# A GEGLU feed-forward kernel: x transposed by the loading transfers instead of by TensorE and VectorE

## The chip, the core and the metric

The kernel runs on one core of one Trainium2 chip. The metric is the device time of one execution in microseconds (us). Before the change the median of 3 runs is 299.68 us (299.42 to 299.73).

The core's parts have these names in the profile: PE is TensorE's matmul (PEld its weight load), DVE is VectorE, ACT is ScalarE, POOL is GpSimd, SP is SyncE, which only issues transfers here. A "q" behind a name (SPq) is that engine's instruction queue where it issues transfers. The transfers of all queues run on the same 16 DMA engines.

## The reference

```python
B, S, D, F = 32, 32, 1024, 3584      # 1024 tokens, all tensors bf16
def reference(x, w_gate, w_up, w_down):
    return (gelu(x @ w_gate) * (x @ w_up)) @ w_down
```

Two products contract over D = 1024, the third over F = 3584.

## The kernel before

It is a hand-ordered program: every engine has its own list of instructions, and semaphores (the `_Clock` objects) tie the lists together. Nothing is scheduled by a tool.

**First stage.** For each chunk m of 128 columns of F (28 chunks) and each group of tokens, TensorE forms gate and up, transposed (F on the partitions, tokens along the rows), in PSUM: 8 steps over the contraction (`dk`), each a matmul of a 128x128 weight block with `xT[:, dk, tokens]` (line 381). ScalarE applies gelu to the gate (line 439), VectorE multiplies with up into `hT` (line 479). The first 8 chunks ("big" weights) are done first for tokens 0 to 255 (parts 0 to 7), then for 256 to 511 (parts 8 to 15), with 256-column matmuls; then their tokens 512 to 1023 and all other chunks with 512-column matmuls. In parts 0 to 7 the loop over `dk` is outside (`together`): all eight chunks take step `dk` for gate and up, so that one weight piece feeds 8 matmuls. Steps 6 and 7 are done in two halves, and step 7 part by part (`one_by_one`). Each accumulates in its own half bank of PSUM.

**Second stage.** The product with `w_down` (line 418), 16 blocks of 128 tokens by 512 columns (the last one in two), each 28 steps; ScalarE and VectorE copy them out in turn, SyncE stores them.

**Where x comes from.** The matmuls need x with the contraction on the partitions. Before the change the contraction index is laid out as `(p k)`: partition p holds rows 8p to 8p+7 of the weights, step `dk` takes one of each eight. x is loaded in its own layout into space in `hT` that is not used yet, and turned in the core:
- tokens 0 to 255 (`xa`, two transfers of 256 KB, one on SyncE's and one on ScalarE's queue, line 292): steps 0 to 4 by ten TensorE matmuls with an identity (line 350), copied from PSUM to `xT` by three ScalarE instructions (line 432); steps 5 to 7 by sixteen VectorE transposes of 32x32 blocks (line 455). The identity is made by POOL (lines 313, 315).
- tokens 256 to 1023 (twelve transfers, half of them on each of two queues, line 283, issued once weight piece `wu` 5 has landed): twenty VectorE transposes (line 470), placed by hand between the VectorE multiplications (`mix`, line 187). Parts 8 to 11 are therefore done in 128-token halves for steps 0 to 3.

**The leading weights.** SyncE issues, one after the other, 16 pieces of 256 KB (line 288): `wg` 0, `wu` 0, `wg` 1, ... `wu` 7; piece k holds step k of the first 8 chunks. Later weights come in groups of four chunks, 1 MB a transfer, gate on SyncE's queue and up on POOL's (line 277); group 0 waits until the last x piece has landed (`gate_w`, line 303), the others until TensorE is done with the buffer. `w_down` is loaded in between (line 271).

**Warming.** Ten matmuls of ones (six of 512 columns, four of 128; line 390) come first on TensorE.

Of the kernel before, what the change touches and what calls it, by code (L numbers as in the profile page):

```python
# [5 lines left out]
P = 128  # L6
BF16 = mybir.dt.bfloat16
FP32 = mybir.dt.float32
ACTF = mybir.ActivationFunctionType
# [75 lines left out]
def bass_standalone__geglu_ffn__sampling_kernel(  # L85
# [13 lines left out]
    DK = D // P  # L99
# [26 lines left out]
    XC = N // 32  # L126
    XE = D // 4
    XA, XB, XC2 = (0, 256), (256, 512), (512, 1024)
    XB1, XB2 = (256, 384), (384, 512)
    XPIECES = [XB1, XB2, XC2]  # L130
    XA_PS = [(3, 0, 1), (4, 1, 3), (5, 3, 5)]
    XA_DVE = (5, 8)
# [25 lines left out]
    def together(ps_, k0, k1, tok=None):  # L158
        for dk in range(k0, k1):
            for key in ("G", "U"):  # L160
                for p in ps_:
                    steps.append((p, key, dk, tok))

    def one_by_one(ps_, k0):
        for p in ps_:
            for key in ("G", "U"):
                for dk in range(k0, DK):
                    steps.append((p, key, dk, None))

    for k0, k1 in ((0, 3), (3, XA_DVE[0])):  # L170
        for b in range(2):
            steps += [("X", b, dk) for dk in range(k0, k1)]
    for key, ps_ in (("G", (0, 1, 2, 3, 7, 6, 4)), ("U", (0, 1, 2, 3)), ("G", (5,)), ("U", (7, 6, 4, 5))):
        steps += [(p, key, 0, None) for p in ps_]
    together(range(0, 8), 1, 6)
    for half in (range(0, 4), range(4, 8)):
        together(half, 6, 7)
        one_by_one(half, 7)
    together(range(8, 12), 0, 4, XB1)
    together(range(8, 12), 0, 4, XB2)  # L180
    together(range(8, 12), 4, 6)
# [3 lines left out]

    dve_order = []
    mix = ("E0 E1 E2 A0 E3 A1 A2 A3 B0 B1 B2 B3 E4 D4 D5 E5 D6 D7 E6 E7 "
           "C0 E8 C1 E9 C2 E10 E11 C3 C4 E12 C5 E13 C6 C7 E14 E15")
    for w in mix.split():
        if w[0] == "E":  # L190
            dve_order.append(("E", int(w[1:])))
        else:
            dve_order.append(("T", int(w[1:])) + {"A": XB1, "B": XB2, "C": XC2, "D": XB}[w[0]])
    dve_order += [("E", p) for p in range(NSHORT, NPART)]
# [14 lines left out]
    xa_r = xf.rearrange("(b p) d -> p b d", p=P)  # L209
    x_r = xf.rearrange("(c i) (a e) -> a i c e", i=32, a=4)  # L210
    wg_r = w_gate.rearrange("(p k) f -> p k f", k=DK)
    wu_r = w_up.rearrange("(p k) f -> p k f", k=DK)
# [5 lines left out]
    C_POOL = _Clock("pool")  # L218
    Q_XA = [_Clock(f"xa{b}", 16) for b in range(2)]
    Q_X = {(q, s): _Clock(f"x{i}{s}", 16) for i, q in enumerate(XPIECES) for s in range(2)}  # L220
    Q_W0 = {(w, k): _Clock(f"{w}0k{k}", 16) for k in range(DK) for w in ("wg", "wu")}
# [5 lines left out]
    all_clocks = [C_PE, C_ACT, C_DVE, C_POOL, *Q_XA, *Q_X.values(), *Q_W0.values(), *Q_WG, *Q_WU,  # L227
# [4 lines left out]
    with ExitStack() as es:  # L232
# [6 lines left out]
        assert 8 * N == XC * XE  # L239
        xs = hT[:, FM - 8:FM, :].rearrange("p a (b e) -> p (a b) e", e=XE)  # L240
        xa = hT[:, FM - 10:FM - 8, :]
        ident = sb("ident", [P, P], BF16)
        diff = sb("diff", [P, P], mybir.dt.int32)
# [36 lines left out]
        def load_x(ew, eng, q, side):  # L280
            c0, c1 = q[0] // 32, q[1] // 32
            for a in (2 * side, 2 * side + 1):
                v = ew.do(lambda: eng.dma_start(
                    xs[32 * a:32 * (a + 1), c0:c1, :], x_r[a, :, c0:c1, :]), clock=Q_X[(q, side)])
            ctx.set(("x", q, side), v)

        def load_w0(ew, eng, w, k):
            ctx.set((w + "0", k), ew.do(lambda: eng.dma_start(  # L288
                big[w][:, k, :], w_r[w][:, k, 0:NBIG * P]), clock=Q_W0[(w, k)]))

        def early_loads(ew, eng, side):
            ctx.set(("xa", side), ew.do(lambda: eng.dma_start(  # L292
                xa[:, side, :], xa_r[:, side, :]), clock=Q_XA[side]))
            yield
            if side == 0:
                for k in range(DK):
                    for w in ("wg", "wu"):
                        load_w0(ew, eng, w, k)
            ew.wait(Q_W0[("wu", 5)], ctx.get(("wu0", 5)))
            for q in XPIECES:  # L300
                load_x(ew, eng, q, side)

        def gate_w(ew, j):
            if war[j] is None:
                for s in range(2):
                    ew.wait(Q_X[(XC2, s)], ctx.get(("x", XC2, s)))
                return -1
            ew.wait(C_PE, ctx.get(("U", last_part[war[j]])))
            return war[j]

        def prog_pool(eng):
            pool = _Eng(ctx, eng, C_POOL)
            v = pool.do(lambda: eng.iota(diff[:, :], pattern=[[1, P]], base=0, channel_multiplier=-1))
            pool.wait(C_POOL, v)
            ctx.set("ident", pool.do(lambda: eng.tensor_scalar(
                ident[:, :], diff[:, :], 0.0, None, ALU.is_equal)))
# [8 lines left out]
        def prog_sp(eng):  # L325
            sp = _Eng(ctx, eng, None)
            for _ in early_loads(sp, eng, 0):
                pass
# [15 lines left out]
        def turn_xa(pe, eng, b, dk):  # L344
            pe.wait(Q_XA[b], ctx.get(("xa", b)))
            j = next(j for j, (_, k0, k1) in enumerate(XA_PS) if k0 <= dk < k1)
            bank, k0, k1 = XA_PS[j]
            o = 256 * (dk - k0) + P * b
            last = dk == k1 - 1 and b == 1
            v = pe.do(lambda: eng.matmul(  # L350
                ps[:, bank, o:o + P],
                xa[:, b, :].rearrange("p (j k) -> p j k", k=DK)[:, :, dk],
                ident[:, :], start=(dk == k0 and b == 0), stop=last), mark=last)
            if last:
                ctx.set(("XP", j), v)

        def part_step(pe, eng, opened, i, key, dk, tok):
            m, t0, t1, gs, us = parts[i]
            w, (bank, f0, f1) = ("wg", gs) if key == "G" else ("wu", us)
            if tok is not None:  # L360
                f0, f1 = f0 + tok[0] - t0, f0 + tok[1] - t0
                t0, t1 = tok
            buf, slot, j = slot_of[m]
            if j is None:
                pe.wait(Q_W0[(w, dk)], ctx.get((w + "0", dk)))
            else:
                pe.wait((Q_WG if w == "wg" else Q_WU)[j], ctx.get((w, j)))
            if bank in bank_before[i]:
                pe.wait(C_DVE, ctx.get(("D", bank_before[i][bank])))
            for jx, (xbank, k0, k1) in enumerate(XA_PS):  # L370
                if t0 == XA[0] and (xbank == bank or k0 <= dk < k1):
                    pe.wait(C_ACT, ctx.get(("XA", jx)))
            if t0 == XA[0] and dk >= XA_DVE[0]:
                pe.wait(C_DVE, ctx.get("XD"))
            for q in XPIECES:
                if q[0] < t1 and t0 < q[1]:
                    pe.wait(C_DVE, ctx.get(("T", dk, q)))
# [12 lines left out]
        WARM = [512] * 6 + [128] * 4  # L390

        def prog_pe(eng):
# [4 lines left out]
            pe.wait(C_POOL, ctx.get("ident"))  # L397
            opened = set()
            for step in steps:
                if step[0] == "X":  # L400
                    turn_xa(pe, eng, *step[1:])
                else:
                    part_step(pe, eng, opened, *step)
# [22 lines left out]
        def prog_act(eng):  # L426
            act = _Eng(ctx, eng, C_ACT)
            act.do(lambda: eng.activation(warm[:, 0:1], const0, ACTF.Gelu_apprx_tanh))
            for _ in early_loads(act, eng, 1):
                for j, (bank, k0, k1) in enumerate(XA_PS):  # L430
                    act.wait(C_PE, ctx.get(("XP", j)))
                    ctx.set(("XA", j), act.do(lambda: eng.activation(  # L432
                        xT[:, k0:k1, XA[0]:XA[1]],
                        ps[:, bank, 0:256 * (k1 - k0)].rearrange("p (k t) -> p k t", t=256), ACTF.Copy)))
# [13 lines left out]
        def prog_dve(eng):  # L448
            dve = _Eng(ctx, eng, C_DVE)

            for b in range(2):
                dve.wait(Q_XA[b], ctx.get(("xa", b)))
            for q in range(4):
                for a in range(4):
                    v = dve.do(lambda: eng.transpose(  # L455
                        xT[32 * a:32 * (a + 1), XA_DVE[0]:XA_DVE[1], XA[0]:XA[1]].rearrange(
                            "p k (b t) -> p k b t", t=P)[:, :, :, 32 * q:32 * (q + 1)],
                        xa[32 * q:32 * (q + 1), :, :].rearrange(
                            "p b (j k) -> p k b j", k=DK)[:, XA_DVE[0]:XA_DVE[1], :, 32 * a:32 * (a + 1)]))
            ctx.set("XD", v)  # L460
            for what in dve_order:
                if what[0] == "T":
                    dk, q = what[1], what[2:]
                    landed = [r for r in XPIECES if q[0] <= r[0] < q[1]]
                    for r in landed:
                        for s in range(2):
                            dve.wait(Q_X[(r, s)], ctx.get(("x", r, s)))
                    src = xs[:, q[0] // 32:q[1] // 32, :].rearrange(
# [3 lines left out]
                    for r in landed:  # L472
                        ctx.set(("T", dk, r), v)
# [63 lines left out]
```

## Time and profile before

| what | from | number |
|---|---|---|
| median of 3 runs | times | 299.68 us |
| span of the profiled execution, first to last instruction | page | 298.2 us |
| median less span | worked out | 1.48 us |
| TensorE busy | page, part 1 | 294.9 us |
| VectorE / ScalarE busy | page, part 1 | 64.3 / 42.2 us |
| first-stage matmuls on the chain from 16.91 us | chain in order of time | 182.50 us |
| second-stage matmuls on the chain | chain in order of time | 96.78 us |
| granted TensorE clock | stretches | 1.00 throughout |
| SyncE's issue of a leading weight piece | line 288 | 0.42 to 0.61 us |
| issue of a piece of x behind the weights | line 283 | 0.33 to 1.33 us |

The time of the profiled execution as a whole is not given beside its span; the span is compared with the median.

The leading weight pieces of the same execution, us from the span's start. Issue is from the timeline, landing is issue plus the time to landing that line 288 shows in a window around the issue:

| piece | issue | landing | piece | issue | landing |
|---|---|---|---|---|---|
| wg 0 | 1.17 | 4.8 | wg 4 | 5.05 | 10.7 |
| wu 0 | 1.64 | 5.7 | wu 4 | 5.70 | 11.4 |
| wg 1 | 2.11 | 6.5 | wg 5 | 6.18 | 12.1 |
| wu 1 | 2.58 | 7.2 | wu 5 | 6.65 | 12.75 |
| wg 2 | 3.06 | 7.95 | wg 6 | 7.13 | 13.4 |
| wu 2 | 3.56 | 8.8 | wu 6 | 7.68 | 14.1 |
| wg 3 | 4.03 | 9.3 | wg 7 | 8.17 | 14.8 |
| wu 3 | 4.51 | 10.0 | wu 7 | 8.66 | 16.86 |

How to read it: a share of busy time is an average over the whole span. What a change is worth is read from the stage that it touches, and there from the wait that ends last. In a row of the timeline the first two numbers are start and duration in us; "x8" is the number of instructions merged into it, and what stands in brackets is how long the engine was idle before and what ended it. A row of the stretches gives start:end, length, the busy time of five engines, the granted clock, the DMA engines' busy share (which can exceed 1 where packets overlap) and GB/s.

### The profile page before, as it was taken

Reading aid. Unit: us, or ns where it says so; the run is one execution under the profiler, and the core shown is the slowest. Engines: PE = TensorE matmul, PEld = TensorE weight load, DVE = VectorE, ACT = ScalarE, POOL = GpSimd, SP = SyncE. Lnnn points to the kernel's source line nnn. Section 1 sums busy time; section 2 is a strip of 40 time slices with the busy share of each in tenths; the row PEclk is TensorE's granted clock in tenths of the full one; section 3 lists DMA queues with packets and bytes.
Section 4 is the critical chain, followed back from the end, with each engine's and each line's share of the span. In section 5 each row is a group of like instructions: output and inputs, shape, how many; then the busy total and the mean of one; then the engine's idle time right before and its main releaser. Section 6 shows DMA issues by size and latency. Waiting matters only on the chain.

```text
span 298.2 us, 3515 instructions
## 1 busy us (share of the span) xinstructions
PE 294.9 (99%) x1552; PEld 149.1 (50%) x1552; DVE 64.3 (22%) x108; ACT 42.2 (14%) x78; POOL 7.9 (3%) x14
## 2 busy tenths in 40 slices
PE   8999999999999999999999999999999999999997
PEld 5889644444444444444444444444444444444446
DVE  4669721111122111122111122110000000000000
ACT  3032211121111121111112111110000000000000
POOL 1001001020000002001000000000000000000000
DMA  7988004856009301943103000000000100010001
GB/s 258 391 197 263 22 2 133 289 186 240 0 0 294 131 0 31 372 162 92 51 0 141 0 2 0 0 0 20 18 18 20 35 18 18 20 35 18 18 20 35
DMA packets 17807, 26.43 MB, mean 89 GB/s; under 512 B 1025, under 2 KB 11393, under 8 KB 17793
## 3 DMA queue, kind: packets, MB, share of 16 engines
q1 hardware_dynamic: 13840, 16.78, 17.2%
q0 software_dynamic: 2176, 8.39, 7.9%
q10 hardware_dynamic: 1776, 1.05, 1.3%
q8 instruction: 12, 0.20, 0.3%
q14 instruction: 3, 0.02, 0.0%
HBM read 24.12 MB, written 2.10 MB: 88 GB/s over the span
## 4 chain that ended last, share of the span: by engine, by line
PE 94%; DMA 3%; SPq 2%; issue 0%; ACT 0%
PE ps L381 61%; PE ps L418 32%; DMA wubig<-in_w_up_dram 3%; SPq L288 2%; SPq L292 0%; ACT xT L445 0%
## 5 line engine op out<-in xcount | busy, mean ns | idle before, releaser
L418 PE MATMUL ps<-wd,hT 128*128 128x512 bf16 (+1 forms) x476 | 96.9, 366 | 0.0
L381 PE MATMUL ps<-xT,wubig 128*128 128x512 bf16 (+2 forms) x400 | 79.8, 336 | 0.3 <-DMA wubig<-in_w_up_dram 0.3
L381 PE MATMUL ps<-xT,wgbig 128*128 128x512 bf16 (+2 forms) x400 | 79.8, 336 | 0.2 <-ACT xT L432 0.2
L418 PEld LDWEIGHTS ps<-wd,hT 128*128 128x128 bf16 x476 | 46.6, 98 | 50.4
L479 DVE TENSOR_TENSOR hT<-tb,ps 128x512 bf16<-128x512 f32 (+1 forms) x64 | 39.0, 616 | 136.6 <-PE ps L381 136.6
L439 ACT ACTIVATE tb<-ps 128x512 f32<-128x512 f32 (+1 forms) x64 | 34.2, 544 | 158.4 <-PE ps L381 156.9
L381 PEld LDWEIGHTS ps<-xT,wubig 128*128 128x128 bf16 x400 | 38.1, 98 | 32.1 <-DMA wubig<-in_w_up_dram 0.7
L381 PEld LDWEIGHTS ps<-xT,wgbig 128*128 128x128 bf16 x400 | 38.0, 98 | 31.6 <-DMA wgbig<-in_w_gate_dram 0.3
L381 PE MATMUL ps<-xT,wgsmall 128*128 128x512 bf16 x128 | 30.2, 379 | 0.0
L381 PE MATMUL ps<-xT,wusmall 128*128 128x512 bf16 x128 | 30.2, 379 | 0.0
L485 DVE CAST xT<-ps 128x512 bf16<-128x512 f32 (+1 forms) x8 | 5.3, 658 | 88.1 <-PE ps L418 88.1
L381 PEld LDWEIGHTS ps<-xT,wusmall 128*128 128x128 bf16 x128 | 12.5, 98 | 15.1
L381 PEld LDWEIGHTS ps<-xT,wgsmall 128*128 128x128 bf16 x128 | 12.5, 98 | 15.1
L445 ACT ACTIVATE xT<-ps 128x512 bf16<-128x512 f32 (+1 forms) x9 | 5.2, 573 | 93.1 <-PE ps L418 93.1
L470 DVE STREAM_TRANSPOSE xT<-hT 128x128 bf16<-128x128 bf16 (+2 forms) x20 | 13.4, 714 | 0.0
L455 DVE STREAM_TRANSPOSE xT<-hT 32x192 bf16<-32x192 bf16 x16 | 8.3, 516 | 4.6 <-DMA hT<-in_x_dram 4.1
L277 POOL DMA_DIRECT2D wubig<-in_w_up_dram x3 | 2.7, 886 | 63.3 <-PE ps L381 63.3
L395 PE MATMUL ps<-const-bfloat16-1.0 128*128 128x512 bf16 (+1 forms) x10 | 3.1, 498 | 0.8 <-PEq L522 0.8
L277 POOL DMA_DIRECT2D wusmall<-in_w_up_dram x2 | 2.0, 992 | 47.3 <-PE ps L381 26.0
L271 POOL DMA_DIRECT2D wd<-in_w_down_dram x3 | 2.3, 764 | 19.1 <-PE ps L381 19.1
L395 PEld LDWEIGHTS ps<-const-bfloat16-1.0 128*128 128x128 bf16 x10 | 1.2, 139 | 2.4 <-issue 2.4
L432 ACT ACTIVATE xT<-ps 128x512 bf16<-128x512 f32 (+1 forms) x3 | 1.4, 526 | 2.2 <-PE ps L350 2.2
(10 smaller groups left out, 4.5 us busy)
## 6 DMA issues: line engine op xcount, KB each, us to landing
wd<-in_w_down_dram SPq DMA_DIRECT2D x4, 1024.0 KB, 11.5
wgbig<-in_w_gate_dram SPq DMA_DIRECT2D x3, 1024.0 KB, 5.6
wubig<-in_w_up_dram POOLq DMA_DIRECT2D x3, 1024.0 KB, 9.7
wd<-in_w_down_dram POOLq DMA_DIRECT2D x3, 1024.0 KB, 11.4
wgbig<-in_w_gate_dram SPq DMA_DIRECT2D x8, 256.0 KB, 5.5
wubig<-in_w_up_dram SPq DMA_DIRECT2D x8, 256.0 KB, 5.6
wgsmall<-in_w_gate_dram SPq DMA_DIRECT2D x2, 1024.0 KB, 5.8
wusmall<-in_w_up_dram POOLq DMA_DIRECT2D x2, 1024.0 KB, 9.7
```

Source lines behind the costliest of these rows:

```text
L271: ew.do(lambda: eng.dma_start(wd[:, a:b, :], wd_r[:, a:b, :]), clock=clock)
L277: ctx.set((w, j), ew.do(lambda: eng.dma_start(wbuf(w, buf)[:, :, 0:gsz * P], w_r[w][:, :, c0 * P:(c0 + gsz) * P]), clock=q))
L288: ctx.set((w + "0", k), ew.do(lambda: eng.dma_start(big[w][:, k, :], w_r[w][:, k, 0:NBIG * P]), clock=Q_W0[(w, k)]))
L381: v = pe.do(lambda: eng.matmul(ps[:, bank, f0:f1], wbuf(w, buf)[:, dk, slot * P:(slot + 1) * P], xT[:, dk, t0:t1], start=first, stop=last ...
L395: pe.do(lambda: eng.matmul(ps[:, 0, 0:n], ones_w, ones_x[:, 0:n], start=True, stop=True), mark=False)
L418: v = pe.do(lambda: eng.matmul(ps[:, b, 0:ncols], hT[:, m, tc * P:(tc + 1) * P], wd[:, m, col0:col0 + ncols], start=(m == 0), stop=(m == F ...
L439: ctx.set(("A", i), act.do(lambda: eng.activation(t_bufs[i % NTB][:, 0:t1 - t0], ps[:, gb, g0:g1], ACTF.Gelu_apprx_tanh)))
L445: ctx.set(("E", ji), act.do(lambda: eng.activation(osb[:, tc, col0:col0 + ncols], ps[:, b, 0:ncols], ACTF.Copy)))
L455: v = dve.do(lambda: eng.transpose(xT[32 * a:32 * (a + 1), XA_DVE[0]:XA_DVE[1], XA[0]:XA[1]].rearrange("p k (b t) -> p k b t", t=P)[:, :, ...
L470: v = dve.do(lambda: eng.transpose(xT[:, dk, q[0]:q[1]].rearrange("p (c i) -> p c i", i=32), src))
L479: ctx.set(("D", i), dve.do(lambda: eng.tensor_tensor(hT[:, m, t0:t1], t_bufs[i % NTB][:, 0:t1 - t0], ps[:, ub, u0:u1], ALU.mult)))
L485: ctx.set(("E", ji), dve.do(lambda: eng.tensor_copy(osb[:, tc, col0:col0 + ncols], ps[:, b, 0:ncols])))
```

## The change

The contraction is laid out as `(k p)`: step k takes rows 128k to 128k+127 of the weights, so that a weight piece is one run of rows, and `xT[:, k, :]` is the transpose of 128 columns of x. All of x is brought in by four transposing transfers straight into `xT`, on SyncE's queue: tokens 0 to 255 for steps 0 to 3 ahead of all weights, for steps 4 to 7 behind `wu` 1, tokens 256 to 511 behind `wu` 5, tokens 512 to 1023 behind `wu` 7. The weight pieces of steps 0 and 1 are halved (four chunks each). TensorE's turning matmuls, ScalarE's copies, VectorE's transposes and the identity are gone; so are ScalarE's transfers and the 128-token halves of parts 8 to 11. Two of the ten warming matmuls go. Nothing else changes: every other instruction is in the same order on its engine.

```diff
-    XPIECES = [XB1, XB2, XC2]
-    XA_PS = [(3, 0, 1), (4, 1, 3), (5, 3, 5)]
-    XA_DVE = (5, 8)
+    XPIECES = [(0, 4, XA), (4, 8, XA), (0, 8, XB), (0, 8, XC2)]
+    XAFTER = {("wu", 1): 1, ("wu", 5): 2, ("wu", 7): 3}
+    W0_HALVED = 2
+    w0_pieces = [(w, k, c) for k in range(8) for w in ("wg", "wu")
+                 for c in ((0, 4), (4, 8))[:2 if k < W0_HALVED else 1]]
+    w0_pieces = [(w, k, c if k < W0_HALVED else (0, NBIG)) for w, k, c in w0_pieces]
...
-    for k0, k1 in ((0, 3), (3, XA_DVE[0])):
-        for b in range(2):
-            steps += [("X", b, dk) for dk in range(k0, k1)]
-    for key, ps_ in (("G", (0, 1, 2, 3, 7, 6, 4)), ("U", (0, 1, 2, 3)), ("G", (5,)), ("U", (7, 6, 4, 5))):
-        steps += [(p, key, 0, None) for p in ps_]
-    together(range(0, 8), 1, 6)
+    together(range(0, 8), 0, 6)
     for half in (range(0, 4), range(4, 8)):
         together(half, 6, 7)
         one_by_one(half, 7)
-    together(range(8, 12), 0, 4, XB1)
-    together(range(8, 12), 0, 4, XB2)
-    together(range(8, 12), 4, 6)
+    together(range(8, 12), 0, 6)
...
-    wg_r = w_gate.rearrange("(p k) f -> p k f", k=DK)
-    wu_r = w_up.rearrange("(p k) f -> p k f", k=DK)
+    wg_r = w_gate.rearrange("(k p) f -> p k f", p=P)
+    wu_r = w_up.rearrange("(k p) f -> p k f", p=P)
...
+        def load_x(ew, eng, i):
+            k0, k1, (t0, t1) = XPIECES[i]
+            ctx.set(("x", i), ew.do(lambda: eng.dma_start_transpose(
+                out=xT[:, k0:k1, t0:t1], in_=xf[t0:t1, k0 * P:k1 * P]), clock=Q_X[i]))
+
+        def load_w0(ew, eng, pc):
+            w, k, (c0, c1) = pc
+            ctx.set(("w0", pc), ew.do(lambda: eng.dma_start(
+                big[w][:, k, c0 * P:c1 * P], w_r[w][:, k, c0 * P:c1 * P]), clock=Q_W0[pc]))
+
+        def early_loads(ew, eng):
+            load_x(ew, eng, 0)
+            for pc in w0_pieces:
+                load_w0(ew, eng, pc)
+                if pc[2][1] == NBIG and pc[:2] in XAFTER:
+                    load_x(ew, eng, XAFTER[pc[:2]])
 
         def gate_w(ew, j):
             if war[j] is None:
-                for s in range(2):
-                    ew.wait(Q_X[(XC2, s)], ctx.get(("x", XC2, s)))
+                ew.wait(Q_X[-1], ctx.get(("x", len(XPIECES) - 1)))
...
-        def part_step(pe, eng, opened, i, key, dk, tok):
+        def part_step(pe, eng, opened, i, key, dk):
...
             if j is None:
-                pe.wait(Q_W0[(w, dk)], ctx.get((w + "0", dk)))
+                pc = next(q for q in w0_pieces if q[:2] == (w, dk) and q[2][0] <= m < q[2][1])
+                pe.wait(Q_W0[pc], ctx.get(("w0", pc)))
...
-            for jx, (xbank, k0, k1) in enumerate(XA_PS):
-                if t0 == XA[0] and (xbank == bank or k0 <= dk < k1):
-                    pe.wait(C_ACT, ctx.get(("XA", jx)))
-            if t0 == XA[0] and dk >= XA_DVE[0]:
-                pe.wait(C_DVE, ctx.get("XD"))
-            for q in XPIECES:
-                if q[0] < t1 and t0 < q[1]:
-                    pe.wait(C_DVE, ctx.get(("T", dk, q)))
+            for q, (k0, k1, (x0, x1)) in enumerate(XPIECES):
+                if k0 <= dk < k1 and x0 < t1 and t0 < x1:
+                    pe.wait(Q_X[q], ctx.get(("x", q)))
...
-        WARM = [512] * 6 + [128] * 4
+        WARM = [512] * 6 + [128] * 2
```

## The prediction

> **What bounds the kernel now.** I read the page's busy times and chain first, then the chain in order of time, then the first 20 us of the timeline, then the stretches of 1 to 5 us in the stage where TensorE (PE) has to wait.
>
> ```profile
> span 298.2 us, 3515 instructions
> ...
> PE 294.9 (99%) x1552; PEld 149.1 (50%) x1552; DVE 64.3 (22%) x108; ACT 42.2 (14%) x78; POOL 7.9 (3%) x14
> ...
> DMA  7988004856009301943103000000000100010001
> ...
> PE 94%; DMA 3%; SPq 2%; issue 0%; ACT 0%
> ```
>
> TensorE is busy for 99% of the span, and the DMA engines are full only in the first three slices (22 us). The chain in order of time says what the 6% are that aren't TensorE:
>
> ```profile
> 8.61 0.04 issue
> 8.66 8.20 DMA wubig<-in_w_up_dram
> 16.86 0.05 issue
> 16.91 182.50 PE ps L381 x951
> 199.40 96.78 PE ps L418 x476
> ```
>
> From 16.91 us to 296.2 us TensorE has no gap: 279.3 us of matmuls. What ends last before that is one transfer, the last leading weight piece (wu, chunk 7), issued at 8.66 and landed at 16.86 us. **So the end of the kernel is the landing of that piece plus a fixed 279.3 us**, as long as every later operand is early. The timeline shows the same place from TensorE's side, and where its first real matmul starts:
>
> ```profile
> 4.93 0.92 PE L381 MATMUL ps<-xT,wgbig 128*128 128x256 bf16 x7 [0.20 <-ACT xT L432]
> ...
> 12.74 3.66 SPq L283 DMA_DIRECT2D hT<-in_x_dram  x6
> ...
> 16.37 0.27 PE L381 MATMUL ps<-xT,wgbig 128*128 128x256 bf16 x1
> 16.90 0.10 PEld L381 LDWEIGHTS ps<-xT,wubig 128*128 128x128 bf16 x1 [0.54 <-DMA wubig<-in_w_up_dram]
> 16.91 0.28 PE L381 MATMUL ps<-xT,wubig 128*128 128x256 bf16 x1 [0.26 <-DMA wubig<-in_w_up_dram]
> ```
>
> The stream wanted that piece at 16.65 us (16.91 less 0.26 of waiting), 11.7 us after its start at 4.93. The SyncE issue at 12.74 waits for wu5, so it also dates the landing of chunk 5: 12.75 us. DMA and TensorE are nearly balanced in this stage. The stretches give the speed of the DMA engines when full: the first is weights in rows of 2 KB, the second x in rows of 512 B:
>
> ```profile
> 7.00:12.00 5.00, 5.00 (x48) 4.49 (x46) 4.72 (x10) 0.00 (x0) 0.00 (x0) 1.00 1.05 395
> 17.70:19.40 1.70, 1.70 (x18) 1.53 (x16) 1.70 (x6) 1.17 (x5) 0.00 (x0) 1.00 1.10 321
> ```
>
> The last three columns are the granted clock, the DMA share and GB/s: 395 for long rows, 321 for short ones, both with the engines full. The profile's span is 298.2 us against a median of 299.68 us, so 1.48 us lie around the span; I add changes of the span to the median.
>
> **The price of a transposing transfer.** No row shows one. The built program gives its tile as 16 rows by 128 columns, so I take 128 bf16 = 256 B as its unit. From the two stretches: 395 GB/s over 16 engines is 24.7 B/ns each, 83.0 ns per 2 KB packet; 321 GB/s is 20.1 B/ns, 25.5 ns per 512 B. The straight line through both costs 37.4 ps per byte, so a 256 B packet takes 25.5 - 9.6 = 15.9 ns, or 257 GB/s (estimate). Per 256 KB: 0.664 us plain, 1.02 us transposing. Bounds: as fast as plain (395 GB/s) below; above, a 256 B packet that costs no less than the 512 B one (25.5 ns, 160 GB/s, 1.63 us per 256 KB). I take 257, nearest to the 512 B rows.
>
> The Trainium skill differs with itself here. DMA: Bandwidth & Descriptors, section "Latency and other measured facts", has 261 GB/s for a transposing kernel, by which the sum below would be 300.8 us. Advanced Engine Details and Errata, section "X-Bar Transpose (TRN2)", calls such transfers as fast as regular ones; no run here shows either, and the second reading is rival B.
>
> **Part by part.**
>
> *The weight queue.* Before wu7 the DMA engines move xa (512 KB), the 16 pieces of 256 KB (4 MB), and part of the rest of x. After, SyncE's one queue carries, in order: x0 (256 KB), chunks 0 and 1, x1 (256 KB), chunks 2 to 5, x2 (512 KB), chunks 6 and 7, x3 (1 MB). Up to wu5 the bytes are the same, with 512 KB of them transposing: 12.75 + 2 x (1.02 - 0.664) = 13.46 us. Then x2, which was behind the weights before and now stands ahead of two chunks: + 2.04 = 15.50. Then four plain pieces: + 4 x 0.664 = 18.16 us. Before it was 16.86, of which 4.11 us went to those four pieces, slowed by x pieces of both queues. **The gate moves by +1.30 us.**
>
> *Does TensorE arrive earlier than that?* Yes, so the gate holds. Its start: wg0 landed at 4.77 us (issue 1.17 + 3.6) as the last of 768 KB; the new first half piece is the last of 384 KB, 256 of them transposing: 4.77 - 384/256 x 0.664 + 0.36 = 4.1 us, 0.8 us earlier. With 11.7 us of stream the last piece would be wanted at 15.8 us. On the way it waits for wg2, landing 7.95 + 0.71 = 8.7 us where it is wanted at 4.1 + 2 x 1.75 = 7.6 (1.75 us a chunk: 16 matmuls of 0.109 us), and for chunks 6 and 7. The 0.8 us won at the front is given back by 9 us and ends as waiting.
>
> *TensorE's transposes (10 matmuls, 3.76 to 4.73 us), the ScalarE copies (L432), the iota, the 0.2 us for xT:* they lie ahead of 16.9 us and are part of that earlier start: nothing by themselves. If the gate were not there they would be worth the 0.8 us.
>
> *VectorE's 36 transposes (13.4 + 8.3 us):* off the path; no TensorE idle time after 16.91. Nothing.
>
> *128-column halves.* 64 matmuls from 19.43 to 23.00 us, 3.57 us, become 32 of 0.109 = 3.49: -0.08 us, on the path.
>
> *SyncE's issues.* 0.43 us each and 0.04 between. Four more pieces and a transfer ahead of wg2: issued at 0.73 + 10 x 0.47 = 5.4 us instead of 3.06. By the rates above, wu1's second half lands at 4.1 + 7 x 0.332 = 6.4 us and x1 at 7.5, its bytes moved by 6.9 (before, 768 KB had been moved 0.6 us ahead of wg0's landing); wg2's bytes can start at about 6.5 (the first ones here came some 1.1 us after the first issue). The queue doesn't run dry, with a cover of 0.4 us. The rows of x issues range from 0.33 to 1.33 us; two slow ones (+1.8) would cost 1.4 us: 302.3 us, inside the range. x2's issue, at about 9.2 us, has 4 us of backlog ahead of it.
>
> *The wait for x3.* Group 0's loads on SyncE and POOL wait for it (before: for the last x piece, 22.4 us). 18.16 less 0.5 of landing, plus 4.1, is about 22 us; only those loads are queued behind, and TensorE needs group 0 after 60 us. Tokens 512 and up are needed at 33.5 us. Covered by 11 us or more.
>
> *The weights' new row order.* Rows of 2 KB (1 KB for halves) either way, other addresses. At 25 to 28 us the 1 KB rows of the group loads run at 385 GB/s, so halves cost nothing. The order itself: between 0 and the gain of rival D.
>
> *The clock.* Warming matmuls end 0.2 us earlier and TensorE then waits some 0.6 us; the granted clock is 1.00 throughout in before, and gaps of 0.5 us left it there. Should the first chunk run at half speed, 1.75 us are lost ahead of a gate with 18.16 - 15.8 = 2.4 us of waiting: covered.
>
> **Sum:** +1.30 - 0.08 = +1.2 us. 299.68 + 1.2 = **300.9 us**.
>
> **Rivals.**
>
> *B, transposes at the plain rate:* wu5 at 12.75, x2 1.33, four pieces 2.66: 16.74 us, -0.12, with the halves -0.2: **299.5 us**. For it: the bytes are no more than before, and the engines can be full at 321 to 395. Against: short packets show 19% less already at 512 B.
>
> *C, slow transposes:* 160 GB/s. 12.75 + 2 x (1.63 - 0.664) + 3.26 + 2.66 = 20.6 us, +3.7: **303.3 us**. Against it: packet cost fell from 83.0 to 25.5 ns as size fell, so some more fall is likely. For it: if the 16 engines have to wait for one another to put a tile together, x1 and x2, standing between plain pieces, pay it twice.
>
> *D, faster:* the place is the stream from wg0's landing to wu7's. Between 4.77 and 12.75 us the pieces came 0.725 us apart, not 0.664: the second queue's xa and a source with 57 KB from partition to partition may have slowed them. If the chunk-wise source and one queue let all 4.46 MB behind that point run at 395 GB/s, transposes too, wu7 lands at 4.77 + 11.3 = 16.05 us: -0.8, with the halves **298.8 us**. It decides from a transposing rate of about 340 GB/s with the rest at 395 and no gaps in the queue (3.67 MB in 9.3 us leave 2.3 us for 0.79 MB of x1 and x2, to land by 16.4). Against: needs both at once.
>
> *E, the transfer isn't pipelined:* each 128 x 128 block pays a whole round like the 128 KB output transfer (1.7 us to landing). 32 blocks ahead of wu7: some 50 us, **350 us**. Against: the weight pieces land 0.7 us apart although each takes 5.5 us from issue to landing, so a queue overlaps its transfers. A gentler reading would also hold SyncE's issues.
>
> That the transfers aren't transposing on the way but by single elements is excluded: the built program holds one transposing instruction per piece.
>
> **How the numbers follow.** The gate is at 14.08 + 4p us for p us per 256 KB, so the forecast's case (300 down to 200 GB/s, p from 0.87 to 1.31) spans 300.3 to 302.1 us. Forecast 0.46, B 0.26, C 0.12, D 0.13, E 0.03. A measurement of this kernel tells 0.2% (0.6 us) from no change: slower 0.46 + 0.12 + 0.03 = 0.61, within 0.26, faster 0.13. The range leaves out D and E (0.16): from B less 0.4 us (half of what D adds), 299.1, to C and 0.3 us, the scatter of the runs shown (299.42 to 299.73), 303.6.
>
> **What would show it.** Right: TensorE's first wait that matters is for wubig, chunk 7, near 18.2 us; more waits at chunks 2 and 6; a first matmul near 4.1; x pieces 1.0 us per 256 KB in the DMA slices; no gap behind 18.2. Wrong: a wait for x itself behind chunk 1, SyncE held in an x issue for over 2 us, DMA slices with holes around x1 or x2, a clock under 1 or 256-column matmuls 0.2 us apart at the front, or a gap at 33 us.

## The result and the profile after

The changed kernel takes 307.54 us (median of 4 runs, 305.46 to 307.9) against 299.71 us of the kernel before on the same chip (4 runs): a ratio of 1.0244, 95% interval 1.0216 to 1.0272. It is slower by 7.8 us where 1.2 us was forecast; the forecast's range ended at 303.6 us.

The page of the kernel after (profiled execution: 307.38 us, span 306.1 us):

```profile
span 306.1 us, 3372 instructions
...
PE 298.5 (98%) x1508; PEld 149.5 (49%) x1508; DVE 44.6 (15%) x72; ACT 41.1 (13%) x75; POOL 7.0 (2%) x12
...
DMA  6998500668301900690401200000100010000001
...
PE 92%; SPq 5%; DMA 2%; issue 0%; ACT 0%
```

TensorE has 44 instructions fewer and is busy 3.6 us longer: some of its matmuls ran slower. VectorE is 19.7 us lighter, since its transposes are gone, and the span still grew by 7.9 us. The chain now has 5% in SyncE's queue (before: 2%). In order of time (start, duration, what; L256 issues x, L261 the leading weights, L323 is the first stage):

```profile
0.74 1.34 SPq L256
...
6.06 1.51 SPq L256
7.57 0.05 issue
7.62 0.57 SPq L261
...
11.88 5.00 SPq L256
...
18.49 4.64 DMA wubig<-in_w_up_dram
23.14 0.05 issue
23.18 184.09 PE ps L323 x919
```

The issue at 7.62 us is that of wg 2; the prediction had it at 5.4 us. The gate is where the prediction put it, the landing of the last leading weight piece (wu, chunk 7), but at 23.14 us: 16.86 before, 18.16 forecast. Behind it stand 184.09 us of first-stage matmuls. Before, that stretch began at the same matmul but also held 32 matmuls more (the 128-token halves); it took 182.50. **So 7.9 us = 6.28 us of gate + 1.59 us behind the gate.** TensorE's timeline shows both:

```profile
5.01 1.89 PE L323 MATMUL ps<-xT,wgbig 128*128 128x256 bf16 x8 [1.30 <-DMA wgbig<-in_w_gate_dram]
...
12.38 1.05 PE L323 MATMUL ps<-xT,wgbig 128*128 128x256 bf16 x8 [1.37 <-DMA wgbig<-in_w_gate_dram]
...
20.99 0.61 PE L323 MATMUL ps<-xT,wgbig 128*128 128x256 bf16 x4 [1.45 <-DMA wgbig<-in_w_gate_dram]
...
23.18 0.28 PE L323 MATMUL ps<-xT,wubig 128*128 128x256 bf16 x1 [0.64 <-DMA wubig<-in_w_up_dram]
```

TensorE waits for chunk 2 (behind x1), chunk 6 (behind x2) and the last piece of chunk 7. The first eight matmuls take 1.89 us, those at 12.38 us 1.05: the front runs at half speed, although the granted clock is shown as 1.00 there (5.0 to 9.9 us). The stretches (length, busy time of five engines, granted clock, DMA share, GB/s) show a transposing transfer in full run, and the clock behind the gate:

```profile
17.00:18.20 1.20, 1.20 (x14) 1.07 (x12) 0.00 (x0) 0.00 (x0) 0.00 (x0) 1.00 1.28 291
...
23.30:26.60 3.30, 3.30 (x18) 2.40 (x17) 1.55 (x4) 1.43 (x4) 0.00 (x0) 0.53 1.13 255
```

The landings against the forecast, each as issue plus time to landing:

| transfer | forecast | after | late by |
|---|---|---|---|
| wg 0, first half | 4.1 | 4.96 | 0.9 |
| wu 1, second half | 6.4 | 8.97 | 2.6 |
| x1 | 7.5 | 9.96 | 2.5 |
| wg 2 | 8.7 | 12.3 | 3.6 |
| wu 5 (seven steps at 0.68 us per 256 KB, the forecast's rate) | 13.46 | 17.09 | 3.6, nothing new |
| x2 behind wu 5 | +2.04 | 20.4, +3.3 | +1.3 |
| wu 7 | 18.16 | 23.14 | 5.0 |

All of the delay is made in two places: ahead of wg 2, where the halves, x0 and x1 stand, and around x2.

### The profile page after: what moved, and what is told of

It is laid out like the page before. It is cut to its first block, busy times and chain, and to the rows that moved or that the text cites. A ratio compares the mean times of both kernels' runs of the same rounds, so it can differ in the third digit from the quotient of the medians.

```text
span 306.1 us, 3372 instructions
## 1 busy us (share of the span) xinstructions
PE 298.5 (98%) x1508; PEld 149.5 (49%) x1508; DVE 44.6 (15%) x72; ACT 41.1 (13%) x75; POOL 7.0 (2%) x12
## 3 DMA queue, kind: packets, MB, share of 16 engines
q1 hardware_dynamic: 20960, 17.83, 19.7%
## 4 chain that ended last, share of the span: by engine, by line
PE 92%; SPq 5%; DMA 2%; issue 0%; ACT 0%
PE ps L323 60%; PE ps L356 32%; SPq L261 3%; SPq L256 3%; DMA wubig<-in_w_up_dram 2%; ACT xT L377 0%
## 5 line engine op out<-in xcount | busy, mean ns | idle before, releaser
L323 PE MATMUL ps<-xT,wgbig 128*128 128x512 bf16 (+1 forms) x384 | 81.8, 352 | 4.1 <-DMA wgbig<-in_w_gate_dram 4.1
L323 PE MATMUL ps<-xT,wubig 128*128 128x512 bf16 (+1 forms) x384 | 81.1, 350 | 0.7 <-DMA wubig<-in_w_up_dram 0.6
L323 PEld LDWEIGHTS ps<-xT,wgbig 128*128 128x128 bf16 x384 | 38.5, 101 | 37.7 <-DMA wgbig<-in_w_gate_dram 5.2
L323 PEld LDWEIGHTS ps<-xT,wubig 128*128 128x128 bf16 x384 | 38.3, 100 | 33.6 <-DMA wubig<-in_w_up_dram 1.1
L323 PE MATMUL ps<-xT,wusmall 128*128 128x512 bf16 x128 | 30.2, 379 | 0.0
L323 PE MATMUL ps<-xT,wgsmall 128*128 128x512 bf16 x128 | 30.2, 379 | 0.0
L323 PEld LDWEIGHTS ps<-xT,wgsmall 128*128 128x128 bf16 x128 | 12.5, 98 | 15.1
L323 PEld LDWEIGHTS ps<-xT,wusmall 128*128 128x128 bf16 x128 | 12.5, 98 | 15.1
L377 ACT ACTIVATE xT<-ps 128x512 bf16<-128x512 f32 (+1 forms) x9 | 5.2, 573 | 93.1 <-PE ps L356 93.1
```

Source lines behind the costliest of these rows:

```text
L323: v = pe.do(lambda: eng.matmul(ps[:, bank, f0:f1], wbuf(w, buf)[:, dk, slot * P:(slot + 1) * P], xT[:, dk, t0:t1], start=first, stop=last ...
L377: ctx.set(("E", ji), act.do(lambda: eng.activation(osb[:, tc, col0:col0 + ncols], ps[:, b, 0:ncols], ACTF.Copy)))
```

## The experiments

"Gate" is the landing of wu 7, with a star where TensorE doesn't wait for it; "against before" is the difference of medians from the kernel before on the same chip (299.58 to 299.95 us there). The candidates in words (the expectations give them letters of their own): **the halves** starve the queue, since 128 KB per SyncE issue of 0.43 us and 0.04 between is 279 GB/s, against 395 when full; **transposing** costs more than its bytes where it stands between plain transfers; **the order**, with x2 ahead of chunks 6 and 7; **the row order** of the weights, slower to read; and **the clock** behind the gate.

| run | what differs | median | against before | gate |
|---|---|---|---|---|
| after | | 307.54 | +7.83 | 23.14 |
| a1 | x not turned, plain transfers | 303.84 | +3.9 | 21.16 |
| a2 | old row order | 306.44 | +6.5 | 23.17 |
| a3 | x2 behind wu 7 | 302.90 | +3.0 | 19.6* |
| a4 | whole pieces | 303.61 | +3.7 | 21.26 |
| c1 | a1 + a4 | 302.24 | +2.4 | 19.7* |
| c2 | a3 + a4 | 301.36 | +1.6 | 18.1* |
| c3 | c2 + four 512-column warming matmuls | 301.40 | +1.6 | 17.92* |
| c4 | c3 with the weights on another queue | 304.51 | +4.7 | 19.2* |
| d1 | c1 with the old row order | 302.18 | +2.6 | 19.0* |
| d2 | before with the new row order | 299.83 | +0.25 | 16.1* |
| d3 | c3 with the old row order | 301.03 | +1.45 | 17.6* |
| d4 | first 256 tokens in one transfer, all else late | 300.67 | +1.1 | 17.1* |
| e1 | before, late x by transposing transfers | 299.67 | -0.1 | 15.4* |
| e2 | after + four warming matmuls | 305.34 | +5.6 | 21.83 |
| e3 | after + fillers in TensorE's waits | 306.23 | +6.5 | 23.35* |
| e4 | c3 with plain transfers | 300.29 | +0.5 | 16.94* |

**a1, plain transfers of x.** `dma_start_transpose` gives way to a plain transfer of as many bytes at the same place in the queue, which reads whole rows of x; the products are of an x that isn't turned.

```diff
-            ... eng.dma_start_transpose(out=xT[:, k0:k1, t0:t1], in_=xf[t0:t1, k0 * P:k1 * P])
+            rows = (slice(0, 128), slice(128, 256), slice(256, 512), slice(512, 1024))[i]
+            b = (1, 1, 2, 4)[i]
+            src = xf[rows, :].rearrange("(p b) (k t) -> p (b k) t", b=b, t=t1 - t0)
+            ... eng.dma_start(xT[:, k0:k1, t0:t1], src)
```

> The four x transfers stay in their places on SyncE's queue with the same bytes, but as plain copies that don't turn x (so the products are of an untransposed x). In the changed kernel the last leading weight piece (wu 7) lands at 23.1 us. Theory T (what costs is that the transfers transpose: engines wait for one another where one begins and where it ends): wu 7 lands at 17 to 18 us, no packet of 2 KB much over 84 ns, total 299.8 to 301. Theory R (the weights' new row order slows the plain pieces): wu 7 lands at 20 us or later, total over 302.5. Theory Q (order and number of issues on the one queue): wu 7 at 19 us or later, since SyncE issues as many pieces in the same order.

The chain of a1:

```profile
13.88 7.28 DMA wubig<-in_w_up_dram
21.16 0.05 issue
21.21 182.42 PE ps L326 x919
```

303.84 us (2 runs). Half of the loss, 3.9 us, is there without any transposing: order and halves together. Theory T, which wanted the gate at 17 to 18 us and no long packets, fails here: single 2 KB packets behind x1 take up to 2.1 us. The stretch behind the gate is 182.42 us, which is before's 182.50 less the 0.08 of the halves that the prediction worked out.

**a2, old row order**, with the changed kernel (the contraction of x and of the weights no longer match).

```diff
-    wg_r = w_gate.rearrange("(k p) f -> p k f", p=P)
+    wg_r = w_gate.rearrange("(p k) f -> p k f", k=DK)
```

> The changed kernel with the weights in the old row order, 8 rows to a partition (the contraction then pairs wrong rows of x and weights). Theory T: no change, wu 7 lands at 22.5 to 23.5 us, total 305 to 308. Theory R: chunks 2 to 5 speed up, wu 7 lands at 20 to 21 us, total 302.5 to 304.5. Theory Q: no change.

The gate stays at 23.17 us, so the row order isn't the cause; 306.44 us is of two runs 1.2 us apart.

**a3, x2 behind the last weight piece.**

```diff
-    XAFTER = {("wu", 1): 1, ("wu", 5): 2, ("wu", 7): 3}
+    XAFTER = {("wu", 1): (1,), ("wu", 7): (2, 3)}
```

> x2 (tokens 256 to 511) is issued behind wu 7 instead of ahead of chunk 6; nothing else. Theory T: one of the two transposing transfers ahead of the gate goes, with its 1.8 us of packets and 1 to 2 us of entering and leaving: wu 7 lands at 19 to 20.5 us, total 302.5 to 304.5, unless TensorE then waits for x2 at parts 8 to 11, 2.3 us behind the gate. Theory Q: the same size, since SyncE's 5.0 us in that issue goes from ahead of chunks 6 and 7. Theory R: only the 1.3 us of plain bytes, wu 7 at 21.5 us, total 306.

The chain of a3:

```profile
8.27 4.74 DMA wubig<-in_w_up_dram
13.01 0.05 issue
13.05 9.57 PE ps L324 x86
```

302.9 us, clock 1.00. What ends last is now chunk 2 (wu 2 at 13.01 us), behind x1; one more wait of 0.4 us follows at 22.6 us, where x2 has just landed (22.94) and VectorE frees a bank (23.06). The order is part; the delay ahead of wg 2 is still there and becomes the gate.

**a4, whole pieces for steps 0 and 1.**

```diff
-    W0_HALVED = 2
+    W0_HALVED = 0
```

> No halved pieces: chunks 0 and 1 come in whole pieces, four issues fewer ahead of x1. Theory Q: SyncE is the limit at the front, all that follows is 4 x 0.47 = 1.9 us earlier, wu 7 lands at 21.2 us, total 305. Theory T: the engines are the limit, wu 7 moves by under 0.7 us (22.5 to 23.1), the first matmul is some 0.4 us later, total 306 to 308.

The chain of a4:

```profile
16.40 4.86 DMA wubig<-in_w_up_dram
21.26 0.05 issue
21.31 182.42 PE ps L323 x919
```

303.61 us: wg 2 lands at 10.34 instead of 12.3 us, the gate 1.9 us earlier, as four issues of 0.47 us would have it (21.2 expected), and the clock stays at 1.00. The halves are part, where the prediction had said the queue doesn't run dry.

**c1, plain transfers and whole pieces**, a1's and a4's edits together.

> Plain x transfers as in the run that didn't turn x, and no halved weight pieces. With halves that run's gate (wu 7) was at 21.2 us; with transposing transfers the halves were worth 1.9 us. Theory of lulls (SyncE's issue of halves leaves the queue without a backlog, and each lull costs a restart; nothing else is slow in plain transfers): wu 7 at 17 to 18 us, total 299.8 to 300.8. Theory of issue time alone: 4 x 0.47 us, wu 7 at 19.3 us, total 302.

302.24 us; wu 7 lands at 19.7 us, 1.6 us ahead of a4. The chain starts at 7.60 us, the landing of wu 0, which one DMA engine finished 1.2 us behind the fifteenth; TensorE then goes on at half speed (granted clock 0.65 from 7.6 to 12.5 us) and has no later DMA wait on the chain. The theory of issue time alone (19.3 us, 302) fits and that of lulls doesn't, though the one late engine is part of the 19.7.

**c2, whole pieces and x2 late**, a3's and a4's edits.

> No halved pieces, and x2 behind wu 7. With x2 late alone the chain went from wu 2 (landed at 13.0 us) without a gap; whole pieces bring it 1.9 us forward. Effects add: wu 2 at 11.1 us, total 301.0. Theory that both cure the same lulls: total 302.5 to 303, no better than x2 late alone.

The chain of c2:

```profile
5.40 0.05 issue
5.45 196.18 PE ps L324 x1024
```

301.36 us. From the landing of wg 0 TensorE doesn't wait for a transfer again. All that is left is a start later than before's 4.93 us, and half speed at the front (some 2.1 us).

**c3, c2 with a longer warm-up.**

```diff
-        WARM = [512] * 6 + [128] * 2
+        WARM = [512] * 10 + [128] * 2
```

> As the kernel with whole pieces and x2 late, with four more warming matmuls of 512 columns (about 1.5 us more), which end near the first landing instead of 1.5 to 2 us before it. In the changed kernel the first 24 real matmuls of 256 columns came 0.21 us apart and not 0.11. Clock theory: those 24 now take 0.11 us each, and where the waits behind them don't take up the difference, up to 2.5 us are won; I expect 1 us. Theory that the waits for weights cover it: the spacing changes, the time by less than 0.5 us.

301.4 us (5 runs), no gain. The matmuls are 0.11 us apart from the first, and the time won ends in waits for wg 1 (0.28) and wg 2 (1.1 to 1.3; it lands at 10.4 us, behind x1). The last 0.3 us is a wait for x2, which stands behind wu 7 here and lands at 21.13 us:

```profile
11.71 9.43 DMA xT<-in_x_dram
21.14 0.14 issue
21.27 179.89 PE ps L324 x896
```

The rest is the prediction's "covered", one stage earlier: speed at the front is worth nothing while chunk 2 is late.

**c4, the weights on ScalarE's queue**, x0 and x1 on SyncE's, x2 and x3 behind wu 7.

```diff
+            load_x(ew, eng, 1)
+            ew.wait(Q_W0[("wu", 7, (0, NBIG))], ctx.get(("w0", ("wu", 7, (0, NBIG)))))
+            load_x(ew, eng, 2)
...
+            for pc in w0_pieces:
+                load_w0(act, eng, pc)
```

> As the kernel with whole pieces and long warming, but the 16 leading weight pieces are issued from ScalarE's queue and x0 and x1 from SyncE's one after the other; x2 and x3 wait on SyncE for the landing of wu 7. Theory that the cost comes from SyncE being held and from the one queue's order: wu 2 lands before 9.5 us, total 299 to 300. Theory that a transposing transfer stops the plain ones on all engines, whatever queue they are on: wu 2 near 11 us, total 300.5 to 301.5.

The timeline of c4:

```profile
11.13 1.89 PE L323 MATMUL ps<-xT,wubig 128*128 128x256 bf16 x8 [2.42 <-DMA wubig<-in_w_up_dram]
```

304.51 us, worse than c3 and than either theory. TensorE waits until 11.1 us for wu 1, which the last two DMA engines land 2.1 and 2.6 us behind the middle one, and x0 lands at 5.5 us (3.79 in after). Part of the time is the clock: 0.51 granted from 11.0 to 14.5 us, behind that wait. Taking x off the weights' queue doesn't take it out of their way; whether a plain x would do the same there, no run shows.

**d1, c1 with the old row order**, and **d2, the kernel before with the new one** (a2's edit and its reverse), and **d3, c3 with the old one**.

> Plain x transfers, whole pieces, and the weights in the old row order (x isn't turned, and rows of x and weights don't match). With the new row order one DMA engine ran up to 2 us behind from wu 0 on: wu 0 landed at 7.6 us, wu 7 at 19.7. Theory R (the new row order makes engines fall behind while the queue starts): the pieces land evenly, wu 0 at 5.5 to 6 us, wu 7 at 17.5 to 18.5 us, total 299.8 to 300.8. Theory not R: wu 7 within 0.5 us of 19.7, total 301.5 to 302.5.

> The kernel before with only the weights' row order changed to the new one (the contraction then pairs wrong rows). Theory R: wu 7 lands 1 to 3 us later than 16.9 us, or a chunk in the middle makes TensorE wait; total 300.5 to 302.5. Theory not R: total within 0.3 us of the kernel before.

> As the kernel with transposing transfers, whole pieces, x2 late and long warming (300.7 to 302.1 us, wg 2 landing at 10.4 us), with the old row order. Theory R: wg 2 lands at 9.5 us or earlier, total 300.0 to 300.7. Theory not R: wg 2 at 10.2 to 10.8 us, total 301 to 302.

d1 302.18 against c1's 302.24, with wu 7 0.7 us earlier, between the two theories; d2 a ratio of 1.0008 (0.9999 to 1.0018); d3 +1.45 against c3's +1.6. That candidate is out: the row order costs nothing that can be measured in the time (0.5 us at most by d2's interval), and rival D, which needed a gain from it, falls too.

**d4, one transposing transfer first**, tokens 0 to 255 in one piece of 512 KB, the rest behind wu 7, so that no plain transfer stands between two transposing ones.

```diff
-    XPIECES = [(0, 4, XA), (4, 8, XA), (0, 8, XB), (0, 8, XC2)]
-    XAFTER = {("wu", 1): 1, ("wu", 5): 2, ("wu", 7): 3}
-    W0_HALVED = 2
+    XPIECES = [(0, 8, XA), (0, 8, XB), (0, 8, XC2)]
+    XAFTER = {("wu", 7): (1, 2)}
+    W0_HALVED = 0
...
+        WARM = [512] * 14 + [128] * 2
```

> Tokens 0 to 255 in one transposing transfer of 512 KB ahead of all weights, whole pieces, the rest of x behind wu 7, warming lengthened to about 6.2 us. Theory T (what costs is each change between plain and transposing packets in the running queue, not the bytes): only one such change is left, at the start; the first real matmul comes at 6.3 to 6.6 us, no wait for weights of over 0.5 us follows, and the total is 299.8 + 1.4 (later start) - 0.3 = 300.9 us. Theory without such a cost: the pieces keep landing 1 us apart at the front and TensorE waits for chunks 1 and 2 as before, total 302 or more.

The chain of d4:

```profile
2.20 4.22 DMA wgbig<-in_w_gate_dram
6.42 0.05 issue
6.46 193.97 PE ps L324 x1024
```

300.67 us (6 runs), ratio 1.0034 (1.0021 to 1.0047): the best of the versions in which all of x comes turned. It pays once, at the start (6.46 us against 4.93), and never waits again.

**e1, the kernel before with the late x turned by its transfers.** Tokens 0 to 255 as before, the rest by two transposing transfers behind wu 7, new row order; VectorE's 20 transposes and the 128-token halves go.

```diff
-    XPIECES = [XB1, XB2, XC2]
+    XPIECES = [XB, XC2]
...
+            ctx.set(("x", q), ew.do(lambda: eng.dma_start_transpose(
+                out=xT[:, :, q[0]:q[1]], in_=xf[q[0]:q[1], :]), clock=Q_X[q]))
```

> The kernel before with the new row order, tokens 0 to 255 turned as before by TensorE and VectorE, and tokens 256 to 1023 by two transposing transfers behind wu 7 on SyncE's queue. Theory T (only what stands ahead of the gate costs): TensorE starts at 4.9 us, wu 7 lands by 16 us without a wait, the 128-column halves are gone: 299.2 to 299.5 us, 0.1 to 0.4 us faster than before. Rival: x2 lands 3 us or more behind wu 7 and TensorE waits for it at 19.0 us, or its beginning holds up wu 7: 299.8 to 300.8 us.

299.67 us against 299.77 (12 and 23 runs), ratio 0.999 (0.9978 to 1.0001). Behind the gate a transposing transfer costs nothing that can be measured here (x2 lands at 18.6 us, in time), and the VectorE work that it saves is worth nothing that can be measured either.

**e2, the changed kernel with c3's warm-up.**

> The changed kernel with four more warming matmuls. Theory that the wait for chunk 2 covers the slow clock at the front: the first 24 matmuls come 0.11 us apart, the wait for wg 2 grows by 2 us or more, wu 7 lands at 23 us again, total 305 to 308. Theory that the front's clock is on the path: 2 us less, under 305.

305.34 us (304.42 and 306.27). The profiled run has its gate at 21.83 us, 1.3 us earlier, but because wg 2 landed at 11.34 instead of 12.3 us; how much of that is chance among the DMA engines two runs can't say. TensorE waits 1.54 us for wg 2 there (1.37 in after), so its faster front is mostly given back. This one stays inconclusive.

**e3, fillers in the changed kernel's waits.** Thirteen matmuls with zero weights ahead of chunks 6 and 7, which add nothing to the sums.

```diff
+            fill = {(0, "G", 6): 7, (0, "U", 6): 2, (0, "U", 7): 4}
+                for _ in range(fill.get(step, 0)):
+                    pe.do(lambda: eng.matmul(ps[:, 0, :], zeros_w[:, :], ones_x, start=False, stop=False))
```

> The changed kernel with 13 matmuls of 512 columns by a block of zeros put into the waits for chunk 6 and for wu 7 (they add nothing to the sums). Clock theory: the granted clock stays 1.00 behind 23 us, the stretch behind the gate is 182.4 us again and not 184.1, total 305.2 to 306.0. Theory that the clock follows something else: clock 0.994 and 307 to 308.

The stretch of 22 to 27 us, first in after, then in e3:

```profile
22.00:27.00 5.00, 4.35 (x24) 2.90 (x22) 1.55 (x4) 1.66 (x5) 0.00 (x0) 0.66 1.05 220
```

```profile
22.00:27.00 5.00, 5.00 (x44) 3.96 (x42) 2.47 (x8) 2.42 (x8) 0.00 (x0) 1.00 1.16 233
```

The granted clock is 1.00 instead of 0.66. The gate is as late as in after (some 23.35 us), and the span behind it is 304.7 - 23.4 = 281.3 us, as in before (298.2 - 16.9), against 306.1 - 23.2 = 282.9 in after. The fillers themselves end 0.3 us after the landing, which takes the total above the expected range. The clock's share is confirmed and is worth 1.6 us in the profiled runs; the medians differ by 1.3 (+6.46 against +7.83), with the clock under 1.00 in one of e3's four runs and in three of after's four.

**e4, c3 with a1's plain transfers**: what transposing costs in a queue that is otherwise as good as before's.

> The kernel with whole pieces, x2 late and long warming (301.4 us), with plain x transfers that don't turn x. Theory T: no drain at x1, the first matmul at 4.9 us, chunk 2 in time, 299.9 to 300.4 us. Theory that the front is slow because one queue starts on it, whatever it carries: 301 to 302 us.

The chain of e4:

```profile
2.08 4.55 DMA wubig<-in_w_up_dram
6.68 2.79 PE ps L327 x24
9.51 10.65 PE ps L327 x96
```

300.29 us (10 runs) against c3's 301.4: 1.1 us for transposing. What is left against before is a wait of 1.0 us for wu 0, which four DMA engines land late. wu 7 lands at 16.94 us. Before the change it was 16.86, but by one engine alone: the other fifteen had landed it by 15.57 us.

## Why the prediction was wrong

The landing of wu 7, one part of the change at a time, from e4 to after:

| step | wu 7 | cost |
|---|---|---|
| e4: whole, plain, x2 late | 16.94 | |
| c1: x2 ahead of chunks 6 and 7 | 19.7 | 2.75, some 1.0 of it at a front that one DMA engine held up (wg 2 at 10.4 us, 9.5 in e4) |
| a4: transposing | 21.26 | 1.6 |
| after: halves | 23.14 | 1.9 |

Each landing is of one profiled execution, and in e4 and c1 TensorE doesn't wait for wu 7: the first rows tell of the queue and not of the time. By the other ways round the costs are alike: transposing 2.0 (a1 to after), halves 1.5 (c1 to a1), x2 3.3 (c3 to a4). In the medians the halves cost 1.4 to 1.5 us (a1 to c1, a3 to c2). Then 1.6 us of clock behind the gate.

Three of the prediction's own signs of being wrong came: an x issue of over 2 us (5.00), 256-column matmuls 0.21 us apart at the front, and a clock under 1.

Point by point:

- **Gate and direction: right.** wu 7, waits at chunks 2 and 6, x2 ahead of the gate, no later wait. Of 1.2 us forecast, 7.8 came.
- **"SyncE's issues": the step that failed first.** It found the queue not running dry, with 0.4 us of cover, and priced the halves at nothing because 1 KB rows move as fast. Its count of issues was right, but x0's and x1's took 1.34 and 1.51 us and not 0.43. So wg 0 went out at 2.13 us (first matmul at 5.01, not 4.1) and wg 2 at 7.62 instead of 5.4. It had named two slow x issues as a risk of 1.4 us. The halves come on top: whole pieces give back 1.9 us (a4). That is four issues of 0.47 us, as expected beforehand. That the queue starves on pieces that come at 279 GB/s is argued from this size; the DMA rate from 4 to 7 us doesn't show it (243 GB/s in after, 309 in a4, but also 252 in e4 with whole pieces).
- **"The price of a transposing transfer": wrong kind of price.** The rate was better than forecast: 291 GB/s in full run against 257. But rate isn't the cost: for the 1 MB of x ahead of the gate, 291 instead of the 321 GB/s of plain rows of 512 B makes 0.3 us (estimate). What the runs show is the sum: 1.6 to 2.0 us in after's order, 1.1 in the best (e4 to c3), and nothing that can be measured when it stands behind the gate (e1). The trace's packet records tell where some of it lies. An x transfer between plain ones begins with 256 B packets of up to 0.9 us (18 ns in full run), which all end together with the last plain packets (wu 1: 5 engines done by 8.0 us, 11 at 8.9). That reads as a drain of the engines at the change of kind. Behind x1 wg 2 needs 2.4 us more. In c3 against e4 wu 1 lands 0.1 us later, x1 takes 1.07 us instead of 0.80, and wg 2 follows after 1.24 us instead of 0.67: most is lost behind x1, little at its start. That this restart belongs to transposing is not shown: 2 KB packets behind x1 take up to 1.3 us in after, but 2.1 us in a1, where x1 is plain. Rival C had the reason (engines waiting for one another) with a rate as its price.
- **x2's term: 3.3 us, not 2.04.** 15 of its engines land at 18.8 to 19.0 us, the sixteenth at 20.4, beside a 16 KB instruction packet that took 1.17 us. That is the forecast's size for 15 engines and 1.4 us for the last one. The prediction misread the same thing before the change: of the 4.11 us of the last four pieces, which it laid to x pieces of both queues, 1.3 us are one late engine of wu 7, and the three pieces ahead of it landed 0.68 us apart.
- **"The clock": half right.** The cold front was covered as said (c3 shows why; e2 fits). But the waits of 1.45 and 0.64 us at the gate were themselves an effect of the change, and behind them the clock went to about 0.5 for 3.3 us (under 1.00 in three of the four runs; a4, with 1.11 and 0.77 us, stayed at 1.00). The prediction had read from before's gaps of 0.5 us that gaps do no harm, and didn't put its own new ones to that test. The Trainium skill, TensorE: Matmul & The Clock Gate, Part 1, has a free-running window of some 3.4 us that decides the clock. The slow stretch of 3.3 us agrees with that length. The same page of the Trainium skill, section "Why this matters for your kernels", advises to keep idle gaps under about 3 us. Here the longest was 1.45, and the clock still fell.
- **Rival B's price fell without its premise.** With plain transfers the time was 303.84 us (a1), not 299.5: halves and order alone lose 3.9.
- **Right:** the weights' row order at nothing (d2), the 0.08 us of the halves (a1, a4), VectorE's work off the path and the wait for x3 covered (e1 and the timeline: no wait behind 23.18), four plain pieces behind x2 at 2.72 us against 2.66. One reading was wrong without harm: the DMA slices of before are full beyond the first 22 us too (8 in the fourth, 9 later), where TensorE doesn't wait.

The Trainium skill, Advanced Engine Details and Errata, section "X-Bar Transpose (TRN2)", which calls such transfers as fast as regular ones, doesn't hold here: 291 GB/s against before's 395. The Trainium skill, DMA: Bandwidth & Descriptors, section "Latency and other measured facts", has 261 GB/s for one kernel whose middle dimension is not contiguous, and about 350 to 400 for the contiguous case. The 291 GB/s are of x2, whole rows of x, and lie between.

What stays open: how the 1.6 to 2.0 us split in after's order, and what makes single engines late. c1 and e4, whose x is plain, have late engines at wu 0 (1.2 us) with no instruction packet near.

## What to carry to other kernels

A transfer's price in a running queue is its rate plus what it does to its neighbours: keep transfers of another kind, and small ones, out of the stretch whose last landing is the gate, and put them behind it, where e1 showed no cost (c3 waited 0.3 us for x2 there). Check for each edit whether the queue stays fed at its issue rate, piece size over issue time. A gate that moves later also creates new waits ahead of it; price what TensorE's clock does behind them.

## What the runs showed of the hardware

- An x transfer's issue holds SyncE: 1.34 us for 256 KB at the start, 5.00 and 5.09 us for 512 KB and 1 MB with transfers ahead (0.43 us for a plain 256 KB piece). With 512 KB at the head of the queue it was 1.39 us (d4). What is queued behind it goes out only then: wg 6 at 16.92 us, still ahead of x2's last bytes.
- With x on SyncE's queue and the weights on ScalarE's, the weights still came late: wu 1 at 11.1 us, 8.1 in c3 (c4). No run has plain x there.
- A transfer lands with its slowest engine: the sixteenth was 1.2 to 1.5 us behind the fifteenth in after (x2), before (wu 7), c1 (wu 0) and e4 (plain x2).
- Where a 16 KB instruction packet begins while x2 is transposing, the 256 B packets in flight stop: in c3 it begins at 18.30 us, and all 21 packets in flight, begun by 18.9 us, last until 20.15 to 20.18. It is alike in a3, d3, d4 and e1 (1.3 to 1.5 us). In before and e4 a plain transfer beside such a packet had one late engine. That the packet is the cause is not shown; no run varies it.
- Two waits of 2.1 us in sum within 4 us were followed by half the clock for 3.3 us in three of after's four runs; with fillers it stayed at 1.00 in three of e3's four. In c4's profiled run a wait of 2.42 us was followed by 0.51 for 3.5 us.
- At the front the granted clock is shown as 1.00 while 256-column matmuls come 0.21 us apart (after); c3's longer warm-up brings them to 0.11. The spacing has to be read there, not the granted clock.
